# A fused gated-attention and expert-choice kernel: the second expert's weight halves, its copies, and one comparison of the routing, in another order

## The chip, the core and the metric

The kernel runs on one core of a Trainium2 chip. The metric is the device time of one launch in microseconds (us), the median of three runs. The profile is one further execution, recorded by the hardware profiler. The engines are PE (matrix products), DVE (vector), ACT (activations and copies), POOL (gathers, scatters and accumulating transfers) and SP (which only issues loads).

## The reference

A gated linear attention over q, k, v, alpha of shape (4 batches, 8 heads, 768 steps, 48) gives x, 3072 tokens by 384. x goes through a mixture of eight experts, each of which takes 384 tokens, in the order of all logits.

```python
for t in range(S):
    state = alpha[:, :, t, :, None] * state + np.einsum('bhd,bhe->bhde', k[:, :, t], v[:, :, t])
    y[:, :, t] = np.einsum('bhd,bhde->bhe', q[:, :, t], state)
...
logits = x @ w_gate
order = np.argsort(-logits.flatten())
for idx in order:
    tok, e = (int(idx) // E, int(idx) % E)
    if assigned[tok] >= 0 or counts[e] >= cap:
        continue
    assigned[tok] = e
    counts[e] += 1
    ...
for e in range(E):
    mask = assigned == e
    h = np.maximum(x[mask] @ w1[e], 0.0)
    out[mask] = h @ w2[e]
```

x is 3072 by 384, w_gate 384 by 8, w1 8 by 384 by 1024, w2 8 by 1024 by 384, all float32.

## The kernel before, in words

The kernel has two parts. The first computes the attention in 24 steps, writes x to memory (`x_dram`) and keeps the logits on the chip. The change does not touch it. The second does routing and experts, interleaved.

**Rounds.** A round of the routing finds the tokens of one expert. `search(i)` narrows down a threshold over the digits of the keys: DVE compares the digits with a ramp (`compare`, result `cmp`), PE counts with narrow matmuls (`rt`), DVE finds the digit (`gt`, `k`, `nd`), and so on for every digit. The first digit's comparison covers 128 x 3072 elements; those of later digits are smaller. `extract(i)` turns the choice into row numbers (`idx`, last line L905) and issues three gathers on POOL that fetch the 384 rows of x (`xr`, three blocks of 128). `update(i)` sets the logits of an expert that is full aside, makes new keys, and starts the next round with its first comparison. The first three rounds follow one another in priority, ahead of the experts' work; a later round is raised in priority at the place where its expert begins.

**Weights.** Each expert's w1 (384 by 1024) and w2 (1024 by 384) come in two halves of 768 KB each, raw into `w1r` and `w2r`, by loads that SP issues in `weights`. For experts from the third on both halves are asked for at once. For the first two, the second halves stand in a list `second_half`; `extract` issues them, with a dependency: w1's after gather 0 has landed, w2's after the last gather (gather 2).

**Splitting.** Matmuls work on a rounded high part and a rest. `split(i, hf)` makes both for one half of an expert's weights: ACT copies the rounded value (`w1hi`, `w2hi`) and its negative (`w1lo`, `w2lo`), each half in two pieces (L954); then POOL issues a transfer that adds the raw weights to the negated copy in memory (`low`, L942), and what is left in `w1lo` or `w2lo` is the rest. `behind(n)` names the instruction after which a piece's copies may be issued: for the second half of the first two experts the last `xh`, and the activations of hidden blocks 0, 2 and 3. For the rows of w2, each piece has its low copy and its high copy next to each other.

**Tokens.** `prep(i)` transposes the gathered rows on PE (`xt`, L991), ACT rounds them (`xh`, L994; the handle of the last is `XA[i]`), DVE takes the rest (`xl`, L996).

**Expert.** F = 1024 is worked through in eight hidden blocks of 128. `ffn1(i, q)` computes one with nine matmuls of 128 x 384 (`h`, L1007: high by high, high by rest, rest by high), then ACT makes the rounded ReLU (`hh`, L1011) and DVE its rest (`hl`, L1012). There are two PSUM buffers for `h`: the matmuls of a block wait until `hh` and `hl` of the block two before have read theirs. `ffn2(i, qs)` adds one hidden block to each of three output blocks of 128 tokens with three matmuls (`y`, L1027). After the eighth, ACT evacuates the output block (`yt`, L1031) and POOL scatters it to the output (L1038).

**Order.** The code of experts is written block by block: hidden block n, then the output matmuls of block n - 2. A list scheduler then gives each engine its order from priorities (order of writing, with routing raised) and modelled readiness; `tc.issue_after(x)` makes what is written inside it stand behind x. So an edit of one constraint can move rows elsewhere, and the tables below show what it does to the order.

Of the kernel before, what the change touches and what calls it, by code (L numbers as in the profile page):

```python
# [24 lines left out]
AF = mybir.ActivationFunctionType  # L25
OP = mybir.AluOpType
# [131 lines left out]
def gla_moe_kernel(ctx, tc, q, k, v, alpha, w_gate, w1, w2, out):  # L158
    nc = tc.nc
# [461 lines left out]
    def weights(i, ei):  # L621
        ev = nc.sync.value_load(ei[0:1, 0:1], min_val=0, max_val=E - 1)
        W1R[i] = wp.tile([128, DB, F], F32, name="w1r")
        W2R[i] = wp.tile([128, FB, Dm], F32, name="w2r")

        def load_w1(hf):
            fs = slice(hf * F // 2, (hf + 1) * F // 2)
            return nc.sync.dma_start(W1R[i][:, :, fs], w1v[bass.ds(ev, 1), :, :, fs].rearrange("e p c f -> p (e c) f"))

        def load_w2(hf):  # L630
            qs = slice(hf * FB // 2, (hf + 1) * FB // 2)
            return nc.sync.dma_start(W2R[i][:, qs], w2v[bass.ds(ev, 1), :, qs].rearrange("e p c d -> p (e c) d"))

        def half(hf):
            return load_w1(hf), load_w2(hf)

        half(0)
        if i > 1:
            half(1)
        else:  # L640
            second_half.extend((load_w1, load_w2))

    def compare(i, d, t):
        nt = 2 ** BITS[t]
# [150 lines left out]
    def update(i):  # L795
# [14 lines left out]
        if i + 2 < E:  # L810
            sg = rw.tile([128, NU], I32, name="sg")
            nc.vector.tensor_scalar(sg, m.bitcast(I32), 31, -2 ** 31, op0=OP.arith_shift_right,
                                    op1=OP.bitwise_or)
            nc.vector.scalar_tensor_tensor(asg, sel, es, asg, op0=OP.mult, op1=OP.add)
            key = rw.tile([128, NU], I32, name="key")
            nc.vector.tensor_tensor(key, m.bitcast(I32), sg, op=OP.bitwise_xor)
            val = rw.tile([128, NU, E], BF, name="val")
            nc.vector.tensor_tensor(val, lw, row(m, E), op=OP.is_equal)
            dig = rw.tile([128, nb, NU], BF, name="dig")
            digits(key, dig, rw, NU)  # L820
            st["dig"] = dig
            with tc.issue_after(st["idx"].ins) if i == 2 else ExitStack():
                for _ in compare(i + 1, dig[:, 0], 0):
                    pass
        else:
            nc.vector.scalar_tensor_tensor(asg, sel, es, asg, op0=OP.mult, op1=OP.add)
            val = rw.tile([128, NU, E], BF, name="val")
            nc.vector.tensor_tensor(val, lw, row(m, E), op=OP.is_equal)
# [34 lines left out]
    def extract(i):  # L863
# [49 lines left out]
                out=XR[i][:, b], out_offset=None, in_=x_dram,  # L913
                in_offset=bass.IndirectOffsetOnAxis(ap=IDX[i][:, b:b + 1], axis=0))

        for n, load_ in enumerate(second_half):
            tc.add_manual_dep(load_(1).ins, gathers[0 if n == 0 else NB - 1].ins.name,
                              mybir.DependencyInfo(mybir.DependencyClass.Sync, mybir.DependencyReason.DATA),
                              reason="rows of the first experts before their later weights")
        second_half.clear()  # L920
# [5 lines left out]
    def split(i, hf):  # L926
# [28 lines left out]

        for n, ix_ in enumerate(cols):
            copies(n, (hi1[ix_], w1r[ix_], 1.0), *([(lo1[ix_], w1r[ix_], -1.0)] * (not first)))
        for n, ix_ in enumerate(rows_):
            copies(2 + n, (lo2[ix_], w2r[ix_], -1.0), *([(hi2[ix_], w2r[ix_], 1.0)] * (not first)))
        if first:  # L960
            for ix_ in rows_:
                copies(0, (hi2[ix_], w2r[ix_], 1.0))
# [33 lines left out]
                nc.vector.tensor_sub(lo[:, :, bs], o, hi[:, :, bs])  # L996
        XH[i], XL[i] = hi, lo

    HH, HA, F1 = {}, {}, {}

    def ffn1(i, q):
        hi, lo = CH[i, q][:2]
        o = fps.tile([128, CAP], F32, name="h", bufs=2)
        n = 0
        for a, x in ((hi, XH[i]), (hi, XL[i]), (lo, XH[i])):
            for d in range(DB):
                F1[i, q] = nc.tensor.matmul(o, a[:, d], x[:, d], start=(n == 0), stop=(n == 3 * DB - 1))  # L1007
                n += 1
        hh = fp.tile([128, CAP], F32R, name="hh", bufs=4)
        hl = fp.tile([128, CAP], F32R, name="hl", bufs=4)  # L1010
        HA[i, q] = nc.scalar.activation(hh, o, AF.Relu)  # L1011
        nc.vector.scalar_tensor_tensor(hl, o, 0.0, hh, op0=OP.max, op1=OP.subtract)  # L1012
        HH[i, q] = hh, hl

    Y, F2 = {}, {}
# [1 line left out]
    def ffn2(i, qs):  # L1017
# [3 lines left out]
        for b in range(NB):  # L1021
            bs = slice(b * 128, (b + 1) * 128)
            for q in qs:
                hi, lo = CH[i, q][2:]
                hh, hl = HH[i, q]
                for n, (a, w) in enumerate(((hh, hi), (hh, lo), (hl, hi))):
                    F2[i, q] = nc.tensor.matmul(Y[b], a[:, bs], w,  # L1027
                                                start=(q == 0 and n == 0), stop=(q == FB - 1 and n == 2))
            if FB - 1 in qs:
                yt = fp.tile([128, Dm], F32, name="yt", bufs=5)  # L1030
                nc.scalar.activation(yt, Y[b], AF.Copy)  # L1031
                pending.append((i, b, yt))

    pending, scattered = [], []
# [11 lines left out]
    for n in range(E * FB + 2):  # L1046
        i, q = divmod(n, FB)
        if i < E:
            if q == 0:
                with tc.high_priority():  # L1050
# [5 lines left out]
                    search(i) if i < E - 1 else search_last(i)  # L1056
                    extract(i)
                    route_priority[0] = tc.cur_priority
                prep(i)
            if q % (FB // 2) == 0:  # L1060
                split(i, 2 * q // FB)
            ffn1(i, q)
        if n >= 2:
# [54 lines left out]
```

## Time and profile before

| | us |
|---|---|
| median of three runs | 418.32 |
| the runs | 417.75, 418.32, 418.52 |
| profiled execution | 418.74 |
| span of its trace | 417.0 |
| mean granted TensorE clock in it | 0.978 |
| busy PE | 390.9 (94%) |
| busy DVE | 282.7 (68%) |
| busy ACT | 215.2 (52%) |
| busy POOL | 190.1 (46%) |

The span runs from the first to the last instruction in the trace; the execution has 1.74 us around it. The times in the trace are counted from the span's start. In rows of the timeline stand the start, the duration, the engine, the line, the operation, and `result<-operands` by the program's names; `x3` means that three like it are drawn together; a bracket at the end holds how long the engine sat idle before, and what released it. SPq and POOLq are the sides of SP and POOL that issue transfers. In the view of transfers a row ends with the KB moved and the us from issue to landing. The clock is the share of full speed that PE was granted.

### The profile page before, as it was taken

To read this page: it belongs to the slowest core of one execution; us is meant where nothing else is said; L and a number is where in the kernel's file an instruction comes from. 1 tells how busy PE (TensorE), PEld (TensorE's weight loads), DVE (VectorE), ACT (ScalarE), POOL (GpSimd) and SP (SyncE) were. 2 spreads that over 40 slices of the span, in tenths; PEclk is the share of its full clock that TensorE was granted. 3 is DMA by queue.
4 is the path that set the end of the run, shared out by engine and by line. 5 is a ranking of instruction groups with operands and counts; after the bars stand their busy time and mean duration, and the time that the engine had idled before them with its cause. 6 is when DMAs were issued, how large, how long until landed. Compare 5 with 4: busy or idle time off the path is not lost.

```text
span 417.0 us, 10031 instructions
## 1 busy us (share of the span) xinstructions
PE 390.9 (94%) x3883; PEld 347.4 (83%) x3883; DVE 282.7 (68%) x849; ACT 215.2 (52%) x382; POOL 190.1 (46%) x209
## 2 busy tenths in 40 slices
PE   7899999999999889989959999999999999999992
PEld 3788889877897547978858999898998999999992
DVE  8889998899984696695783797786966941312210
ACT  3456556645652026456536529529628539568211
POOL 4799988666841025144234117245252263614102
PEclk9899999999999999999995999999999999999997
DMA  8989898762022059769899965999998999989601
GB/s 283 362 276 318 264 317 241 236 186 98 18 78 78 2 183 236 149 211 232 222 243 302 210 237 174 193 261 326 211 326 213 209 323 351 241 226 194 157 0 57
DMA packets 43711, 88.05 MB, mean 211 GB/s; under 512 B 3856, under 2 KB 18192, under 8 KB 43664
## 3 DMA queue, kind: packets, MB, share of 16 engines
q1 hardware_dynamic: 32256, 53.60, 38.1%
q0 software_dynamic: 11408, 33.83, 38.1%
q8 instruction: 30, 0.49, 0.5%
q14 instruction: 17, 0.14, 0.1%
HBM read 53.59 MB, written 9.44 MB: 151 GB/s over the span
## 4 chain that ended last, share of the span: by engine, by line
PE 55%; issue 14%; DVE 14%; DMA 12%; POOL 3%; ACT 0%; POOLq 0%; DVEq 0%; ACTq 0%
PE h L1007 14%; PE y L1027 13%; PE xt L391 4%; PE s L403 4%; PE y L454 4%; DMA w1lo<-w1r 4%; PE y L447 4%; DMA w2r<-in_moe_w_dram 3%; DMA w2lo<-w2r 3%; DVE te L363 2%; PE rt L707 2%; PE lg L472 2%; PE rt L710 2%; DVE tp L369 2%; POOL out_dram L1038 2%
## 5 line engine op out<-in xcount | busy, mean ns | idle before, releaser
L1011 ACT ACTIVATE hh<-h 128x384 fp32r<-128x384 f32 x64 | 31.3, 489 | 89.5 <-PE h L1007 73.5
L1027 PE MATMUL y<-w2lo,hh 128*128 128x384 f32 x192 | 65.8, 343 | 4.1 <-DMA w2lo<-w2r 4.1
L1012 DVE SCALAR_TENSOR_TENSOR hl<-h,hh 128x384 fp32r<-128x384 f32 x64 | 35.2, 553 | 50.5 <-ACT hh L1011 50.0
L1027 PE MATMUL y<-w2hi,hh 128*128 128x384 f32 x192 | 66.8, 348 | 0.0
L1027 PE MATMUL y<-w2hi,hl 128*128 128x384 f32 x192 | 65.5, 347 | 0.0
L912 POOL DMA_INDIRECT xr<-x_dram,idx x24 | 32.1, 1338 | 57.3 <-DVE idx L905 22.8
L1007 PE MATMUL h<-xh,w1hi 128*128 128x384 f32 x192 | 47.2, 350 | 1.9 <-DVE hl L1012 1.9
L1007 PE MATMUL h<-xh,w1lo 128*128 128x384 f32 x192 | 47.3, 346 | 0.3 <-DMA w1lo<-w1r 0.3
L1038 POOL DMA_INDIRECT out_dram<-yt,idx x24 | 24.8, 1032 | 48.5 <-ACT yt L1031 44.6
L1007 PE MATMUL h<-xl,w1hi 128*128 128x384 f32 x192 | 46.4, 347 | 0.0
L1027 PEld LDWEIGHTS y<-w2lo,hh 128*128 128x128 f32 x192 | 36.6, 191 | 4.4 <-DMA w2lo<-w2r 4.4
L942 POOL DMA_DIRECT2D w1lo<-w1r x15 | 20.6, 1372 | 41.2 <-ACT w1lo L954 39.3
L373 POOL TENSOR_TENSOR kh<-rk,te 128x512 f32<-128x512 f32 (+1 forms) x24 | 29.4, 1227 | 18.7 <-DVE z L383 11.3
L1007 PEld LDWEIGHTS h<-xh,w1hi 128*128 128x128 f32 x192 | 34.1, 193 | 3.4 <-DVE hl L1012 2.2
L1027 PEld LDWEIGHTS y<-w2hi,hh 128*128 128x128 f32 x192 | 36.6, 191 | 0.0
L1027 PEld LDWEIGHTS y<-w2hi,hl 128*128 128x128 f32 x192 | 36.5, 191 | 0.1
L1007 PEld LDWEIGHTS h<-xl,w1hi 128*128 128x128 f32 x192 | 34.7, 193 | 0.8 <-DVE xl L996 0.2
L1007 PEld LDWEIGHTS h<-xh,w1lo 128*128 128x128 f32 x192 | 34.5, 191 | 0.5 <-DMA w1lo<-w1r 0.4
L650 DVE TENSOR_TENSOR cmp<-nd,iota 128x1536 bf16<-128x1536 bf16 (+3 forms) x32 | 32.7, 1032 | 0.9
L405 ACT ACTIVATE sm<-s 128x1024 f32<-128x1024 f32 x24 | 24.6, 1024 | 14.0 <-PE s L403 13.8
L369 DVE TENSOR_TENSOR_SCAN tp<-al,z 128x512 f32<-128x512 f32 (+1 forms) x26 | 29.6, 1138 | 2.6 <-DVE z L383 0.5
L363 DVE TENSOR_TENSOR_SCAN te<-al,z 128x511 f32<-128x511 f32 (+2 forms) x26 | 30.9, 1187 | 0.5
(191 smaller groups left out, 830.8 us busy)
## 6 DMA issues: line engine op xcount, KB each, us to landing
w1r<-in_moe_w_dram SPq DMA_DIRECT2D x16, 768.0 KB, 12.6
w2r<-in_moe_w_dram SPq DMA_DIRECT2D x16, 768.0 KB, 14.1
w2lo<-w2r POOLq DMA_DIRECT2D x16, 768.0 KB, 10.7
w1lo<-w1r POOLq DMA_DIRECT2D x15, 768.0 KB, 8.9
al<-in_alpha_dram SPq DMA_DIRECT2D x24, 260.0 KB, 4.2
rk<-in_k_dram SPq DMA_DIRECT2D x24, 256.0 KB, 4.3
rq<-in_q_dram SPq DMA_DIRECT2D x24, 256.0 KB, 4.4
rv<-in_v_dram SPq DMA_DIRECT2D x24, 192.0 KB, 4.1
```

The lines of the kernel that those rows point to most:

```text
L363: nc.vector.tensor_tensor_scan(te.t[:, lo:top][:, ::-1], al.t[:, lo + 1:top + 1][:, ::-1], zb[:, lo + 1:top + 1][:, ::-1], al.t[:, 4 * C + ...
L369: nc.vector.tensor_tensor_scan(tp.t[:, lo:hi], al.t[:, lo:hi], zb[:, lo:hi], 1.0, op0=OP.mult, op1=OP.add)
L373: eng.tensor_tensor(out_.t[:, us].rearrange("p u c -> p (u c)"), x.t[:, lo:hi], f.t[:, lo:hi], op=OP.mult)
L405: add(A_, 1.05, lambda: nc.scalar.activation(sm.t, sc.t, AF.Copy), r=[(sc, 0), (sc, 1)], w=[sm])
L650: nc.vector.tensor_tensor(words(dst, nt, js), keyed(d, nt, js), each(iotas[t], nt, js), op=OP.is_ge)
L912: gathers[b] = last_gather[0] = nc.gpsimd.indirect_dma_start(out=XR[i][:, b], out_offset=None, in_=x_dram, in_offset=bass.IndirectOffsetOn ...
L942: return nc.gpsimd.dma_start(x.bitcast(F32), raw_, accum_op=OP.add, max_dma_last_dim=8192)
L1007: F1[i, q] = nc.tensor.matmul(o, a[:, d], x[:, d], start=(n == 0), stop=(n == 3 * DB - 1))
L1011: HA[i, q] = nc.scalar.activation(hh, o, AF.Relu)
L1012: nc.vector.scalar_tensor_tensor(hl, o, 0.0, hh, op0=OP.max, op1=OP.subtract)
L1027: F2[i, q] = nc.tensor.matmul(Y[b], a[:, bs], w, start=(q == 0 and n == 0), stop=(q == FB - 1 and n == 2))
L1038: st_ = nc.gpsimd.indirect_dma_start(out=out, out_offset=bass.IndirectOffsetOnAxis(ap=IDX[i][:, b:b + 1], axis=0), in_=yt, in_offset=None)
```

## The change

1. `weights`: for the second expert (i = 1), w1's second half is asked for at once, behind the first halves of w1 and w2, and w2's second half after gather 0 in place of gather 2. The first expert keeps its order.
2. `update(1)`: the first comparison of the third round (of expert 2, counted from 0) stands behind `hl` of the first expert's seventh hidden block. `ffn1` keeps the handle of `hl` in `HL` for that.
3. `split(1, 1)`: the copies of w2 are listed as both low copies (behind hidden block 2's activation) and then both high copies (behind block 3's), in place of low and high for each piece.
4. `ffn2`: the first expert's evacuations stand behind the second expert's last `xh`.
5. The main loop calls `split(1, 0)` ahead of `prep(1)`, not behind it.

```diff
--- before.py
+++ after.py
@@ -637,8 +637,11 @@
         half(0)
         if i > 1:
             half(1)
+        elif i:
+            load_w1(1)
+            second_half.append((load_w2, 0))
         else:
-            second_half.extend((load_w1, load_w2))
+            second_half.extend(((load_w1, 0), (load_w2, NB - 1)))
 
     def compare(i, d, t):
         nt = 2 ** BITS[t]
@@ -819,7 +822,8 @@
             dig = rw.tile([128, nb, NU], BF, name="dig")
             digits(key, dig, rw, NU)
             st["dig"] = dig
-            with tc.issue_after(st["idx"].ins) if i == 2 else ExitStack():
+            behind = {1: HL.get((0, FB - 2)), 2: st["idx"]}.get(i)
+            with tc.issue_after(behind.ins) if behind is not None else ExitStack():
                 for _ in compare(i + 1, dig[:, 0], 0):
                     pass
         else:
@@ -913,8 +917,8 @@
                 out=XR[i][:, b], out_offset=None, in_=x_dram,
                 in_offset=bass.IndirectOffsetOnAxis(ap=IDX[i][:, b:b + 1], axis=0))
 
-        for n, load_ in enumerate(second_half):
-            tc.add_manual_dep(load_(1).ins, gathers[0 if n == 0 else NB - 1].ins.name,
+        for load_, b in second_half:
+            tc.add_manual_dep(load_(1).ins, gathers[b].ins.name,
                               mybir.DependencyInfo(mybir.DependencyClass.Sync, mybir.DependencyReason.DATA),
                               reason="rows of the first experts before their later weights")
         second_half.clear()
@@ -955,8 +959,12 @@
 
         for n, ix_ in enumerate(cols):
             copies(n, (hi1[ix_], w1r[ix_], 1.0), *([(lo1[ix_], w1r[ix_], -1.0)] * (not first)))
-        for n, ix_ in enumerate(rows_):
-            copies(2 + n, (lo2[ix_], w2r[ix_], -1.0), *([(hi2[ix_], w2r[ix_], 1.0)] * (not first)))
+        if i == 1 and hf:
+            copies(2, *((lo2[ix_], w2r[ix_], -1.0) for ix_ in rows_))
+            copies(3, *((hi2[ix_], w2r[ix_], 1.0) for ix_ in rows_))
+        else:
+            for n, ix_ in enumerate(rows_):
+                copies(2 + n, (lo2[ix_], w2r[ix_], -1.0), *([(hi2[ix_], w2r[ix_], 1.0)] * (not first)))
         if first:
             for ix_ in rows_:
                 copies(0, (hi2[ix_], w2r[ix_], 1.0))
@@ -996,7 +1004,7 @@
                 nc.vector.tensor_sub(lo[:, :, bs], o, hi[:, :, bs])
         XH[i], XL[i] = hi, lo
 
-    HH, HA, F1 = {}, {}, {}
+    HH, HA, F1, HL = {}, {}, {}, {}
 
     def ffn1(i, q):
         hi, lo = CH[i, q][:2]
@@ -1009,7 +1017,7 @@
         hh = fp.tile([128, CAP], F32R, name="hh", bufs=4)
         hl = fp.tile([128, CAP], F32R, name="hl", bufs=4)
         HA[i, q] = nc.scalar.activation(hh, o, AF.Relu)
-        nc.vector.scalar_tensor_tensor(hl, o, 0.0, hh, op0=OP.max, op1=OP.subtract)
+        HL[i, q] = nc.vector.scalar_tensor_tensor(hl, o, 0.0, hh, op0=OP.max, op1=OP.subtract)
         HH[i, q] = hh, hl
 
     Y, F2 = {}, {}
@@ -1028,7 +1036,8 @@
                                                 start=(q == 0 and n == 0), stop=(q == FB - 1 and n == 2))
             if FB - 1 in qs:
                 yt = fp.tile([128, Dm], F32, name="yt", bufs=5)
-                nc.scalar.activation(yt, Y[b], AF.Copy)
+                with tc.issue_after(XA[1].ins) if i == 0 else ExitStack():
+                    nc.scalar.activation(yt, Y[b], AF.Copy)
                 pending.append((i, b, yt))
 
     pending, scattered = [], []
@@ -1056,8 +1065,10 @@
                     search(i) if i < E - 1 else search_last(i)
                     extract(i)
                     route_priority[0] = tc.cur_priority
+                if i == 1:
+                    split(i, 0)
                 prep(i)
-            if q % (FB // 2) == 0:
+            if q % (FB // 2) == 0 and n != FB:
                 split(i, 2 * q // FB)
             ffn1(i, q)
         if n >= 2:
```

What this does to the order is shown at three places. The first is DVE around the first comparison of the third round, `cmp_101<-dig`, while the first expert's last hidden blocks are worked on; `chu`, `rem` and `o` are the last steps of `update`, `gt` and `k` the search's next ones. Before:

```order
L836 TENSOR_TENSOR chu<-ch,un 128x24
L837 SCALAR_TENSOR_TENSOR rem<-cl,rem 128x8
L650 TENSOR_TENSOR cmp_101<-dig,iota 128x3072
L839 TENSOR_TENSOR o<-ramp_b,chu 128x192
L1012 SCALAR_TENSOR_TENSOR hl<-h,hh 128x384 x2
L717 TENSOR_TENSOR gt_97<-rt,rem 128x8
L729 TENSOR_REDUCE k<-rt 128x1
```

And after:

```order
L840 TENSOR_TENSOR chu<-ch,un 128x24
L841 SCALAR_TENSOR_TENSOR rem<-cl,rem 128x8
L1020 SCALAR_TENSOR_TENSOR hl<-h,hh 128x384
L843 TENSOR_TENSOR o<-ramp_b,chu 128x192
L1020 SCALAR_TENSOR_TENSOR hl<-h,hh 128x384
L653 TENSOR_TENSOR cmp_101<-dig,iota 128x3072
L1020 SCALAR_TENSOR_TENSOR hl<-h,hh 128x384
L720 TENSOR_TENSOR gt_97<-rt,rem 128x8
L732 TENSOR_REDUCE k<-rt 128x1
```

Two residuals now stand ahead of the comparison. In two later rounds the order moves one residual the other way, from ahead of the round's `sums` or `lw` to behind that round's first comparison.

The second place is ACT at the second expert's second half of weights (`w2lo`, `w2hi`; `hh` are activations of its hidden blocks, `yt` the last evacuation of the first expert). Before:

```order
L1031 ACTIVATE yt<-y_2284 128x384
L1011 ACTIVATE hh<-h 128x384
L954 ACTIVATE w2lo<-w2r 128x768
L954 ACTIVATE w2hi<-w2r 128x768
L1011 ACTIVATE hh<-h 128x384
L954 ACTIVATE w2lo<-w2r 128x768
L954 ACTIVATE w2hi<-w2r 128x768
L1011 ACTIVATE hh<-h 128x384
```

And after:

```order
L1019 ACTIVATE hh<-h 128x384
L958 ACTIVATE w1lo<-w1r 128x3x256
L1019 ACTIVATE hh<-h 128x384
L958 ACTIVATE w2lo<-w2r 128x768 x2
L1019 ACTIVATE hh<-h 128x384
L958 ACTIVATE w2hi<-w2r 128x768 x2
L1019 ACTIVATE hh<-h 128x384 x2
```

Both low copies now follow one activation; the last evacuation has moved up, ahead of the copies of w1. On POOL all three scatters of the first expert now stand ahead of the second half's accumulate into `w1lo`; before, it was two, and one behind it.

The third place is PE at the second expert's second and third hidden block (`y_2284` is the first expert's last output block, `y_2768` the second expert's first). Before:

```order
L725 LDWEIGHTS one_84
L725 MATMUL rt<-gt_97,one_84 128x8
L1007 MATMUL h<-xh,w1lo 128x384 x2
L1027 MATMUL y_2284<-w2lo,hh 128x384
L1027 MATMUL y_2284<-w2hi,hl 128x384
L1007 MATMUL h<-xh,w1hi 128x384 x3
L1007 MATMUL h<-xl,w1hi 128x384 x2
```

And after:

```order
L728 LDWEIGHTS one_84
L728 MATMUL rt<-gt_97,one_84 128x8
L1015 MATMUL h<-xh,w1lo 128x384 x3
L1035 MATMUL y_2768<-w2hi,hh 128x384
L1035 MATMUL y_2768<-w2lo,hh 128x384
L1015 MATMUL h<-xh,w1hi 128x384 x3
L1015 MATMUL h<-xl,w1hi 128x384 x3
```

The first expert's output matmuls are all done earlier, ahead of the second expert's first hidden block, and the second expert's own first two have taken their place. A little earlier on PE, the transposes of the second expert's first block stand ahead of the 24 narrow matmuls of the comparison; before, they followed them.

## The prediction

> **What bounds the kernel now.** I read the page's busy times first, then TensorE's (PE's) waits by what ended them, then busy time in single stretches beside the granted clock, and last the timeline around each wait.
>
> ```profile
> PE 390.9 (94%) x3883; PEld 347.4 (83%) x3883; DVE 282.7 (68%) x849; ACT 215.2 (52%) x382; POOL 190.1 (46%) x209
> ```
> PE is busy for 94% of the span, so only PE's idle time and its clock can be won. In the part from 120 us to the end, where all edits lie, the waits of the expert matmuls are these three (us in total, times, longest):
> ```profile
> PE y L1027 <- DMA w2lo<-w2r: 4.1, 1, 4.1
> PE h L1007 <- DVE hl L1012: 1.9, 1, 1.9
> PE h L1007 <- DMA w1lo<-w1r: 0.3, 1, 0.3
> ```
> The next view gives, for a stretch, its length, the busy time of PE, weight load, DVE, ACT and POOL, the granted clock, the DMA share and GB/s:
> ```profile
> 9.37:12.79 3.42, 1.45 (x28) 1.14 (x25) 3.27 (x9) 1.40 (x4) 2.91 (x4) 1.00 1.08 382
> 12.79:16.20 3.41, 3.41 (x30) 2.71 (x25) 3.24 (x8) 0.64 (x2) 2.31 (x3) 0.50 1.05 367
> 183.45:186.87 3.42, 1.92 (x11) 1.60 (x10) 3.42 (x12) 3.42 (x5) 3.12 (x2) 1.00 0.71 254
> 214.17:217.59 3.42, 0.75 (x5) 0.43 (x3) 2.99 (x5) 2.49 (x4) 2.61 (x2) 1.00 1.05 233
> 217.59:227.83 10.24, 8.84 (x49) 7.92 (x50) 2.89 (x5) 6.46 (x9) 4.16 (x4) 0.50 1.07 313
> 342.00:390.00 48.00, 48.00 (x292) 47.08 (x291) 12.01 (x25) 35.05 (x59) 18.80 (x18) 1.00 1.03 254
> ```
> The wait of 4.1 us costs twice: behind the window that it empties (0.75 of 3.42 busy) PE runs at half clock for 10.24 us, and 8.84 us of work there would have taken half, 4.42 us. The last row shows the later experts: no idle, nothing to win, but any new delay is paid in full. The start 12.79 and the start 217.59 of the half clock lie 204.8 us apart, 60 times 3.413: the clock is decided in fixed windows of that length. A window 0.42 busy (1.45 of 3.42) lost the clock, one 0.56 busy (1.92) kept it. I take the threshold between, at 1.5 to 2.0 us idle in one window.
>
> The Trainium skill, "TensorE: Matmul & The Clock Gate", section "Why this matters for your kernels", asks for no PE gap above about 3 us, since one window of idle brings the half clock back. The 4.07 us wait agrees with that; the first window, with 28 matmuls in it, loses the clock all the same, so the measurement is the stricter one. By the page alone, no wait that I expect below would cost clock, and rival A would fall away.
>
> **The change, part by part.** All against the profiled execution, 418.74 us (span 417.0, 1.74 around it); the median is 418.32, 0.42 lower.
>
> *Comparison behind a residual.* Now the third round's first comparison stands ahead of two residuals on DVE, and the eighth hidden block's matmuls wait for one of them:
> ```profile
> 184.73 1.75 DVE L650 TENSOR_TENSOR cmp<-dig,iota 128x3072 bf16<-128x3072 bf16 x1
> 186.67 1.01 DVE L1012 SCALAR_TENSOR_TENSOR hl<-h,hh 128x384 fp32r<-128x384 f32 x2
> 187.28 0.79 PE L1007 MATMUL h<-xh,w1hi 128*128 128x384 f32 x3 [1.91 <-DVE hl L1012]
> ```
> The new order has two residuals first, about 1.0 us; the 1.75 us comparison no longer stands in PE's way: **+1.91** (1.5 to 1.91). The comparison itself comes about 1 us later; behind it on DVE stand the round's next steps, whose matmuls are filled in between expert matmuls.
>
> *Request order and copies.* The second expert's second halves, now:
> ```profile
> 187.06 0.37 SPq L628 DMA_DIRECT2D w1r<-in_moe_w_dram  x1
> 191.82 0.37 SPq L632 DMA_DIRECT2D w2r<-in_moe_w_dram  x1
> w2r<-in_moe_w_dram SPq DMA_DIRECT2D x1, 768.0 KB, 13.1
> 201.92 0.49 ACT L1011 ACTIVATE hh<-h 128x384 fp32r<-128x384 f32 x1 [1.58 <-PE rt L725]
> 205.04 0.84 ACT L954 ACTIVATE w2lo<-w2r 128x768 fp32r<-128x768 f32 x1 [2.63 <-DMA w2r<-in_moe_w_dram]
> 208.04 0.91 POOL L942 DMA_DIRECT2D w2lo<-w2r  x1 [5.56 <-ACT w2lo L954]
> w2lo<-w2r POOLq DMA_DIRECT2D x1, 768.0 KB, 10.9
> 218.99 0.69 PE L1027 MATMUL y<-w2lo,hh 128*128 128x384 f32 x1 [4.07 <-DMA w2lo<-w2r]
> ```
> The w2 load leaves SP when the third gather lands (191.82) and arrives at 204.9 (13.1 later). With gather 0 as its condition it leaves at 187.06, where w1's left, and by the same 13.1 arrives by 200.2. ACT then needs only the activation that the copies stand behind (201.92, done 202.41) and the two low copies side by side (2 x 0.84): POOL can issue at 204.1 instead of 208.04. At the same 10.9 the low half lands at 215.0, where PE wants it at 218.99 - 4.07 = 214.92. PE's own gains move both ends alike. So **+4.07** (3.4 to 4.07), and the high copies, now last, follow one activation later, still long before that use. With the wait the emptied window goes, and the half clock: **+4.42** (0 to 4.42, nothing if another window takes its place).
>
> *w1's second half at once.* SP sends it right behind the first halves, ahead of the gathers of x:
> ```profile
> w1r<-in_moe_w_dram SPq DMA_DIRECT2D x1, 768.0 KB, 4.7
> w2r<-in_moe_w_dram SPq DMA_DIRECT2D x1, 768.0 KB, 6.2
> 181.98 1.09 POOL L912 DMA_INDIRECT xr<-x_dram,idx  x1 [8.06 <-DVE idx L905]
> xr<-x_dram,idx POOLq DMA_INDIRECT x1, 5.1
> 188.95 0.96 PE L707 MATMUL rt<-o,cmp 128*128 128x8 bf16 x24
> 190.50 0.82 PE L991 MATMUL xt<-ident,xr 128*128 128x128 f32 x6
> ```
> The second of two loads took 1.5 us more than the first (6.2 against 4.7), so gather 0 may land up to 1.5 us after its 187.1 (181.98 + 5.1). The first transposes now stand ahead of the 24 narrow matmuls and reach PE at 190.50 - 1.91 - 0.96 = 187.6. **-0.5** (0 to 1.0). The w2 load's start moves with that gather; at 1.5 us later it still arrives before 201.92.
>
> *Split and evacuations.* The first expert's three evacuations stand behind the third xh now, and the new order puts no output matmuls between the last transposes and the second expert's first hidden block (four before):
> ```profile
> 194.19 0.49 PE L991 MATMUL xt<-ident,xr 128*128 128x128 f32 x3
> 195.33 0.77 PE L1007 MATMUL h<-xh,w1hi 128*128 128x384 f32 x3
> ```
> From the transposes' end (194.68) to the matmul that uses their xh (195.33): **-0.65** (0.3 to 0.7), uncovered. Next, the second expert's first two output matmuls stand ahead of its third hidden block instead of behind it:
> ```profile
> 188.92 1.06 POOL L942 DMA_DIRECT2D w2lo<-w2r  x1
> w2lo<-w2r POOLq DMA_DIRECT2D x1, 768.0 KB, 11.7
> 202.02 0.34 PE L1027 MATMUL y<-w2lo,hh 128*128 128x384 f32 x1
> ```
> They reach PE at about 202.02 - 2.0 (nine wide at 48.00 / 292 = 0.164, and twelve narrow at 0.04) - 0.76 (1.91 less the 1.15 above) = 199.3; the low half lands at 188.92 + 11.7 = 200.6 at the latest. **-1.2** (0 to 1.9). The third scatter now stands ahead of the low half of w1 on POOL, and that half's 0.3 us wait could stay or double: **-0.3** (0 to 0.7).
>
> *What is late next.* PE reaches the third expert sooner, its weights don't come sooner: their low halves are issued behind gathers that follow the round's idx.
> ```profile
> 214.24 0.16 DVE L905 SCALAR_TENSOR_TENSOR idx<-xt,other 64x3 int32<-64x3 f32 x1
> 219.67 1.46 POOL L942 DMA_DIRECT2D w1lo<-w1r  x1
> w1lo<-w1r POOLq DMA_DIRECT2D x1, 768.0 KB, 10.2
> 236.74 0.34 PE L1007 MATMUL h<-xh,w1lo 128*128 128x384 f32 x1
> 252.10 0.16 DVE L905 SCALAR_TENSOR_TENSOR idx<-xt,other 64x3 int32<-64x3 f32 x1
> 258.15 1.44 POOL L942 DMA_DIRECT2D w1lo<-w1r  x1
> w1lo<-w1r POOLq DMA_DIRECT2D x1, 768.0 KB, 6.9
> ```
> From idx to use it is 22.5 us now; both big gains fall inside it (8.5), and the new order leaves 7 wide and 12 narrow matmuls fewer in between (1.6): 12.3. From idx to landing took 15.6 here (5.4 + 10.2) and 13.0 for the fourth expert (6.0 + 6.9). So a new wait of 0.7 to 3.3; I take a little above the middle, since the first row is the same expert: **-2.2**. In two later rounds the new DVE order moves one residual from ahead of the round's sums to behind the first comparison, as it stood in the case just mended:
> ```profile
> 300.21 1.76 DVE L650 TENSOR_TENSOR cmp<-dig,iota 128x3072 bf16<-128x3072 bf16 x1
> ```
> Each may cost nothing or a comparison's 1.8; I take 1.7 for the one at this row and half, 0.8, for the earlier one: **-2.5** (0 to 3.6).
>
> Sum: 1.91 + 4.07 + 4.42 = 10.40 won; 0.5 + 0.65 + 1.2 + 0.3 + 2.2 + 2.5 = 7.35 given back; net 3.05. 418.74 - 3.05 = 415.7 for a profiled execution, **415.3** on the median. Half-widths added in squares give 2.5 to either side: 412.8 to 417.8.
>
> **Rivals.**
> A, the half clock comes back. The new wait at the third expert's first low half empties a window. It decides where 1.5 to 2.0 us of one window are idle; then three windows at half clock cost about 4.4 again: 415.3 + 4.4 = 419.7, slower. For it: a wait of 2.2 us lies in a window at random, and has 1.75 of it in one window with a chance of (3.41 - 2.2 + 2 x 0.45) / 3.41 = 0.6. Against: only about half of the waits that I allow there are that long.
> B, most waits that I fear are covered: the later residuals cost nothing (2.5 back) and the third expert's weights come as fast as the fourth's did (0.6 instead of 2.2). Net 7.15: 411.2. For it: the later rows at 342 to 390 show no idle at all under the same structure. Against: the 1.91 us case is just such a residual.
> C, the change doesn't do what it says: the w2 load, though sooner asked for, arrives no sooner, since it shares the DMAs with w1's half and the low accumulates (shares of 1.05 and 1.07 in the windows above), or the low half takes 4 us longer in flight. Then the 4.07 and 4.42 stay, and 1.91 pays for 0.5 + 0.65 + 0.3, and for the rest little is asked since PE is as late as before: 418.3.
>
> **How the numbers follow.** Three runs from 417.75 to 418.52 tell 0.2%, 0.84 us, from no change: "same" is 417.5 to 419.2. Forecast 0.53 (0.50 of it faster, 0.03 same); A 0.27, since half of the 0.8 that B and C leave, times 0.6, is about a quarter (spread 417.0 to 420.8: 0.05 faster, 0.09 same, 0.13 slower); B 0.13, faster; C 0.07 (0.04 same, 0.03 slower). Faster 0.68, same 0.16, slower 0.16. The range 411.0 to 420.0 leaves out some 0.05 of B, 0.08 of A and 0.03 of the forecast.
>
> **What the changed profile would show.** Right: no wait of h on hl near 185; the w2 load of the second expert leaving near 187, two low copies in a row on ACT, and the low accumulate issued before 205; no y wait on w2lo above 0.7 and a clock of 1.00 from 214 to 225; a wait of h on w1lo of about 2 us at the third expert. Wrong: slices of half clock anywhere after 180 (A); no wait above 0.5 after 222 (B); the 4 us wait still there (C). What would upset all of it is a wait on the gathers near 187 longer than 1 us, because everything of the second expert stands behind it.

## The result, and the profile after

In the first set of runs the changed kernel took 420.29 us (median of 20, 417.74 to 422.80) against 417.12 us of the kernel before (20 runs, 413.45 to 422.49): a ratio of 1.0092, interval 1.0067 to 1.0117. The forecast was 415.3 us. Two more sets of runs gave 0.9999 (0.9968 to 1.0029) and 1.0032 (0.9997 to 1.0067). The kernel before, run against itself, gave 1.0005, 0.9944 and 0.9991, so a set of runs can be off by some 0.5%. The ratios leave out runs more than 1.5% above the fastest of their kernel and aren't quotients of the medians; by the medians of all runs the three sets of the change give 1.0076, 0.9981 and 1.0009. So no set shows a gain clear of noise, and the first shows a loss of 0.8 to 0.9%.

The profiled execution of the changed kernel took 417.74 us (span 416.0), the shortest of its 20; that of the kernel before, 418.74, lies 1.6 above the median of the 20 runs. The two profiles alone would say "1 us faster".

From the page of the profile after, busy times and the granted clock in 40 equal slices of the span (a digit is tenths of full speed, 9 is 90% or more):
```profile
PE 388.0 (93%) x3883; PEld 345.2 (83%) x3883; DVE 282.7 (68%) x849; ACT 214.2 (51%) x382; POOL 189.7 (46%) x209
PEclk9899999999999999999999998999999999999997
```
The waits of PE after, from 120 us on (us in total, times, longest), those of the experts and rounds that grew or are new:
```profile
PE rt L710 <- DVE cmp L653: 3.7, 1, 3.7
PE h L1015 <- DVE hl L1020: 1.3, 1, 1.3
PE xt L999 <- DMA xr<-x_dram,idx: 1.2, 1, 1.2
PE y L1035 <- DMA w2lo<-w2r: 0.7, 1, 0.7
PE h L1015 <- ACT xh L1002: 0.6, 1, 0.6
```
The waits of 4.1 and 1.9 us are gone, and five others of 7.5 us in all stand in their place. The residual first (timeline after):
```profile
185.11 0.79 PE L1015 MATMUL h<-xh,w1hi 128*128 128x384 f32 x3
185.71 1.74 DVE L653 TENSOR_TENSOR cmp<-dig,iota 128x3072 bf16<-128x3072 bf16 x1
```
The hidden block starts before the comparison does. Then the low half of w2, request to use:
```profile
188.65 0.37 SPq L632 DMA_DIRECT2D w2r<-in_moe_w_dram  x1
203.37 1.57 ACT L958 ACTIVATE w2lo<-w2r 128x768 fp32r<-128x768 f32 x2
205.25 0.93 POOL L946 DMA_DIRECT2D w2lo<-w2r  x1 [2.54 <-ACT w2lo L958]
w2lo<-w2r POOLq DMA_DIRECT2D x1, 768.0 KB, 7.1
216.72 0.33 PE L1035 MATMUL y<-w2lo,hh 128*128 128x384 f32 x1
```
The two low copies stand together, the accumulate leaves 2.8 us sooner than before (208.04) and lands at 212.3, 4.4 us ahead of its use. The new large wait lies in the round of the fifth expert (the fourth expert's row numbers, and the second digit's comparison behind them), while the third expert is computed. PE, ACT and DVE there, in order of time:
```profile
244.60 0.68 PE L1015 MATMUL h<-xh,w1lo 128*128 128x384 f32 x3
245.58 0.85 ACT L958 ACTIVATE w1hi<-w1r 128x768 fp32r<-128x768 f32 x1 [4.33 <-DMA w1r<-in_moe_w_dram]
249.27 0.46 ACT L1019 ACTIVATE hh<-h 128x384 fp32r<-128x384 f32 x1
249.76 0.56 DVE L1020 SCALAR_TENSOR_TENSOR hl<-h,hh 128x384 fp32r<-128x384 f32 x1 [4.37 <-ACT hh L1019]
250.91 0.16 DVE L909 SCALAR_TENSOR_TENSOR idx<-xt,other 64x3 int32<-64x3 f32 x1
251.11 1.76 DVE L653 TENSOR_TENSOR cmp<-nd,iota 128x3072 bf16<-128x3072 bf16 x1
252.92 0.96 PE L710 MATMUL rt<-o,cmp 128*128 128x8 bf16 x24 [3.65 <-DVE cmp L653]
```
The hidden block is complete at 245.3. ACT serves it at 249.27, because five of the fourth expert's copies stand ahead in ACT's queue: the first waits 4.33 us for its raw weights, and the five then take from 245.58 to 249.27. Before, the same five copies started at 249.81 without a wait and ended at 253.49, when a hidden block had just been completed (253.16). The residual waits for that activation, the row numbers stand behind the residual on DVE, the comparison behind the row numbers, and PE stands in front of the counts of that comparison. The clock follows; busy times and clock by windows:
```profile
246.68:250.09 3.41, 2.59 (x15) 2.27 (x14) 0.33 (x1) 3.41 (x6) 1.16 (x1) 1.00 1.04 384
250.09:253.51 3.42, 0.59 (x17) 0.59 (x18) 3.06 (x7) 3.42 (x6) 2.38 (x2) 1.00 0.94 183
253.51:256.92 3.41, 3.41 (x22) 3.10 (x20) 1.37 (x5) 2.46 (x4) 2.81 (x4) 0.50 0.88 201
```

### The profile page after: what moved, and what is told of

Read it like the earlier page. It is cut to its first block, busy times and chain, and to the rows that moved or that the text cites. A ratio compares the mean times of both kernels' runs of the same rounds, so it can differ in the third digit from the quotient of the medians.

```text
span 416.0 us, 10032 instructions
## 1 busy us (share of the span) xinstructions
PE 388.0 (93%) x3883; PEld 345.2 (83%) x3883; DVE 282.7 (68%) x849; ACT 214.2 (51%) x382; POOL 189.7 (46%) x209
## 4 chain that ended last, share of the span: by engine, by line
PE 52%; DVE 17%; issue 14%; DMA 10%; POOL 3%; ACT 1%; POOLq 0%; SPq 0%; DVEq 0%; ACTq 0%
PE h L1015 13%; PE y L1035 12%; PE xt L391 4%; PE y L447 4%; PE y L454 4%; DMA w1lo<-w1r 4%; PE s L403 4%; DMA w1r<-in_moe_w_dram 3%; DMA w2lo<-w2r 3%; DVE te L363 3%; PE lg L472 2%; PE rt L710 2%; PE rt L713 2%; DVE tp L369 2%; POOL out_dram L1047 2%
## 5 line engine op out<-in xcount | busy, mean ns | idle before, releaser
L916 POOL DMA_INDIRECT xr<-x_dram,idx x24 | 30.6, 1275 | 57.9 <-DVE idx L909 29.4
L1047 POOL DMA_INDIRECT out_dram<-yt,idx x24 | 25.8, 1074 | 48.6 <-ACT yt L1040 44.4
L1015 PE MATMUL h<-xl,w1hi 128*128 128x384 f32 x192 | 45.1, 340 | 0.0
L958 ACT ACTIVATE w1hi<-w1r 128x768 fp32r<-128x768 f32 x32 | 26.8, 840 | 9.8 <-DMA w1r<-in_moe_w_dram 7.4
```

The costliest lines, as they stand in the source:

```text
L916: gathers[b] = last_gather[0] = nc.gpsimd.indirect_dma_start(out=XR[i][:, b], out_offset=None, in_=x_dram, in_offset=bass.IndirectOffsetOn ...
L958: nc.scalar.activation(dst, src, AF.Copy, scale=scale)
L1047: st_ = nc.gpsimd.indirect_dma_start(out=out, out_offset=bass.IndirectOffsetOnAxis(ap=IDX[i][:, b:b + 1], axis=0), in_=yt, in_offset=None)
```

## The experiments

All are timed against the kernel before in the same set of runs. Two figures help to read them. The clock loss of a run is 1 minus its mean granted clock, times its span: the time that a PE that is always busy loses to half clock. The rest is the run's time less that. The table has the medians of both over all runs. The waits are those of PE on experts and rounds from 176 to 400 us, added up in the one trace of each kernel.

| kernel | median, before in the same set | ratio (interval) | clock loss | rest | waits |
|---|---|---|---|---|---|
| loads_copies | 419.91, 422.49 | 0.9952 (0.9919 to 0.9985) | 7.1 | 413.8 | 6.9 |
| residual_only | 421.78, 422.49 | 0.9997 (0.9961 to 1.0033) | 5.9 | 415.8 | 9.2 |
| all_but_residual | 421.09, 422.49 | 0.9977 (0.9940 to 1.0014) | 8.2 | 413.5 | 7.0 |
| change_again | 421.68, 422.49 | 0.9999 (0.9968 to 1.0029) | 6.5 | 416.2 | 8.5 |
| before_again | 422.26, 422.24 | 1.0005 (0.9959 to 1.0052) | 10.1 | 412.8 | 7.1 |
| change_copies_later | 420.05, 422.24 | 0.9967 (0.9935 to 0.9999) | 5.9 | 414.3 | 7.6 |
| loads_copies_later | 423.24, 422.24 | 1.0028 (0.9989 to 1.0067) | 9.1 | 414.3 | 9.0 |
| before_copies_later | 427.55, 422.24 | 1.0152 (1.0104 to 1.0200) | 10.2 | 417.5 | 10.6 |
| change_w1_behind_gather | 421.97, 417.70 | 1.0101 (1.0052 to 1.0150) | 8.2 | 413.8 | 9.1 |
| change_all_copies_later | 419.02, 417.70 | 1.0022 (0.9986 to 1.0059) | 6.1 | 413.0 | 6.5 |
| change_sixth_residual | 418.10, 417.70 | 1.0012 (0.9981 to 1.0043) | 5.8 | 412.7 | 5.8 |
| change_all_three | 419.29, 417.70 | 1.0066 (1.0029 to 1.0103) | 7.5 | 412.1 | 6.2 |
| change_two_placements | 414.61, 418.38 | 0.9915 (0.9877 to 0.9953) | 3.7 | 410.8 | 3.4 |
| change_third | 418.76, 418.38 | 1.0032 (0.9997 to 1.0067) | 6.0 | 413.3 | 6.8 |
| loads_copies_again | 416.66, 418.38 | 0.9960 (0.9914 to 1.0006) | 5.6 | 410.3 | 4.5 |
| before_third | 416.65, 418.38 | 0.9944 (0.9892 to 0.9996) | 6.2 | 410.7 | 4.7 |
| two_placements_again | 416.15, 422.18 | 0.9884 (0.9823 to 0.9946) | 4.8 | 411.7 | 5.2 |
| before_fourth | 421.87, 422.18 | 0.9991 (0.9951 to 1.0031) | 8.8 | 413.0 | 6.9 |

There were six sets of runs. In three of them the kernel before takes 422.2 to 422.5 us, in the others 417.1 to 418.4; the last section says what the traces show of that. The chip alone doesn't explain it: two sets are recorded on chip 3, and before takes 417.70 us in one and 422.18 in the other. The difference isn't the same for every kernel, so ratios of different sets are compared with care.

### Which part moves the order

In the programs' order, the new requests and the paired copies alone leave PE and DVE as they were before. The comparison behind the residual alone changes both, in later rounds too: counted from the first expert, the row numbers of the fourth, fifth and sixth expert then stand behind 22, 29 and 35 residuals on DVE, before behind 21, 28 and 34. So the first four kernels part the two.

**Loads and copies alone** (`weights`, `extract` and the copies of `split` from the change, all else from before).

> Only the request order of the second expert's loads and its paired low copies; the order on PE and DVE stays that of before. Theory 1 (the loss comes from the order that the comparison behind a residual brings to the fourth expert's round, where row numbers and the second digit's comparison now stand behind one more residual): the 4.07 us wait on w2lo goes with its half clock, the 1.91 us wait on the residual stays, no wait on a comparison above 0.5 us near 250; 3 to 6 us faster than before. Theory 2 (whatever PE gains early is given back to later weights and rounds): the 4 us go, but waits of the same sum appear behind 220; within 1.5 us of before.

**Residual alone** (`behind` in `update`, with `HL`).

> Only the comparison behind the residual; loads, copies, evacuations and split as before. Theory 1: the 1.91 us wait is gone, the 4 us wait on w2lo stays with its half clock, and near 250 PE waits 1 to 3.7 us for the second digit's comparison; 0 to 3 us slower than before. Theory 2: nothing but the 1.91 us changes; 1 to 2 us faster.

**All but the residual** (`update` as before, the rest as in the change).

> The whole change without the comparison behind the residual. Theory 1: as with loads and copies alone, 3 to 6 us faster than before, so 6 to 9 faster than the whole change; no wait on a comparison near 250. Theory 2: near the whole change, 1 to 4 us slower than before, with waits on weights or row numbers behind 220.

**The whole change again.**

> The whole change once more, for a second trace. Theory 1: the wait of 3 to 4 us on the second digit's comparison near 250 is there again, and half clock follows it; 2 to 4 us slower than before. Theory 3 (which windows the clock loses is chance, and no wait of the change's own decides): the wait is there or not, and the half clock lies at other places; the time differs from the first profile's by up to 4 us.

The residual alone took 1.9 us less wait at its place and more elsewhere: rest 415.8 against before's 413.5 in that set (35 runs). The new waits are 3.0 us on the second expert's w1 low half near 198, 1.6 behind a residual at 224 and 1.9 on the comparison near 255. The wait on w2lo, expected to stay, is gone. Loads and copies alone were faster, by 2.6 us where 3 to 6 were expected, and all but the residual by 1.4, within the bounds of no change. So theory 1 was right on the side that makes things worse, but most of the wait that loads and copies remove comes back too, with the old order: 6.9 us of waits in all, against 7.1 in before_again. The largest of those that are new, in the timeline of loads_copies:
```profile
246.27 0.85 ACT L957 ACTIVATE w1hi<-w1r 128x768 fp32r<-128x768 f32 x1 [2.47 <-DMA w1r<-in_moe_w_dram]
249.96 0.47 ACT L1017 ACTIVATE hh<-h 128x384 fp32r<-128x384 f32 x1
250.46 0.56 DVE L1018 SCALAR_TENSOR_TENSOR hl<-h,hh 128x384 fp32r<-128x384 f32 x1 [2.53 <-ACT hh L1017]
250.93 0.15 DVE L720 TENSOR_TENSOR gt<-rt,rem 128x8 bf16<-128x8 f32 x1
251.14 0.17 PE L728 MATMUL rt<-gt,one 128*128 128x8 bf16 x1 [1.45 <-DVE gt L720]
```
It is the same ACT queue: copies that wait for the fourth expert's raw weights hold up an activation, that a residual, that a step of the round. In the old order only `gt` stands behind that residual, since the row numbers came one residual sooner; in the new one the row numbers and the comparison do, and the price is 3.0 to 3.7 us in place of 1.45. In the first trace of before PE completes that hidden block 8 us later (253.16 against 245.28) and waits for nothing.

### Is it the copies on ACT?

One number changes, for the fourth expert (i = 3):
```diff
-            return HA[i - 1, SPLIT_AFTER[i > 1]] if i and not hf else None
+            return HA[i - 1, 5 if i == 3 else SPLIT_AFTER[i > 1]] if i and not hf else None
```
`SPLIT_AFTER[1]` is 4, so the copies now follow the activation that they held up.

> The kernel before once more, for a second trace. Both theories below: the 4.07 us wait on w2lo near 215 and the 1.9 us wait on the residual are there again, and no wait above 1 us between 240 and 260. How long the half clock lasts behind the first is open: 3.4 us (one window) or 10.2 us (three); if it differs from trace to trace, the time of this kernel varies by some 3 us for that alone.

> The whole change, and the fourth expert's weight copies (first half) stand behind the third expert's sixth activation on ACT in place of its fifth. Theory A (those copies, waiting for weights that land near 245.6, keep the sixth activation waiting on ACT, it the residual on DVE, that the row numbers and the second digit's comparison, and PE): the wait of 3 to 3.7 us near 250 falls below 1 us and its half clock goes; 3 to 6 us faster than the whole change, so 2 to 6 us faster than before. Theory B (the round itself takes that long once PE is early, whatever ACT does): the wait stays above 2 us or shows at the next step of the same round; within 1.5 us of the whole change.

> Loads and paired copies alone, with the same one placement of the fourth expert's copies. Theory A: the 1.45 us wait near 251 goes with its window of half clock; 1.5 to 4 us faster than loads and copies alone, so 3 to 6 us faster than before. Theory B: a wait of 1 us or more stays at that round; within 1 us of loads and copies alone.

> The kernel before with that one placement and nothing else. Theory A: PE reaches the fourth expert's round some 8 us later there and never waits for it, so within 1 us of before. If the placement is good by itself, whatever PE does: 2 us or more faster than before.

In the changed kernel the wait near 250 is gone, as theory A says, and the time fell from 0.9999 to 0.9967 of before's; that is 1.4 us, not 3 to 6, and across two sets. A wait with the same cause came one expert later, since the fifth expert's copies wait 3.22 us for their weights on ACT:
```profile
281.24 0.17 PE L728 MATMUL rt<-gt,one 128*128 128x8 bf16 x1 [2.21 <-DVE gt L720]
```
With the old order the same edit does harm: in loads_copies_later and before_copies_later it moves a residual behind a comparison, and a new wait of 2.35 us on `hl` stands at 268 and 275. Theory A's "within 1 us" for before was wrong: it became 5.3 us slower, since the edit moves PE's and DVE's order also where no wait was. Loads and copies alone, for which 1.5 to 4 us of gain were expected, lost too. This pair doesn't test the cause; the changed kernel does.

### Each wait at its own place

Three edits on the whole change, one by one and together:
```diff
-            load_w1(1)
-            second_half.append((load_w2, 0))
+            second_half.extend(((load_w1, 0), (load_w2, 0)))
```
```diff
-            return HA[i - 1, SPLIT_AFTER[i > 1]] if i and not hf else None
+            return HA[i - 1, 5 if i > 2 else SPLIT_AFTER[i > 1]] if i and not hf else None
```
```diff
-            behind = {1: HL.get((0, FB - 2)), 2: st["idx"]}.get(i)
+            behind = {1: HL.get((0, FB - 2)), 2: st["idx"], 5: HL.get((4, 0))}.get(i)
```

> The whole change, but the second expert's second half of w1 is asked for behind gather 0 again (w2's second half right after it); the order on every other engine is that of the change. Theory A (each wait stands where its own cause is, and leaves with it): the wait of 1.2 to 1.4 us on the gathered rows near 189 goes and no other grows; 1 to 1.5 us faster than the whole change. Theory B (what is won at one place is waited for at the next routing step or weight): within 0.7 us of the whole change, or slower, with a wait on w1lo or w2lo near 205 to 217.

> The whole change, with the copies of the first half of every expert from the fourth on placed one activation later (the fourth alone was tried before and moved a wait of 2.2 us to 281). Theory A: no wait above 1 us at 250 or at 281; 3 to 5 us faster than the whole change. Theory B: a wait of 1 to 3 us stays at one of these rounds, or weights come too late for their first use; within 1.5 us of the version with the fourth expert's copies alone, or slower than it.

> The whole change, with the same placement for the round of the seventh expert: its first comparison behind the fifth expert's first residual. Theory A: the wait of 1.3 us on that residual near 302 goes, the one near 250 stays; 1 to 1.5 us faster than the whole change. Theory B: the later comparison makes the round late, and PE waits at 305 to 312 for it by 1 us or more over the whole change; within 0.7 us of it.

> The three edits together on the whole change. Theory A: the gains add to 5 to 8 us, so 1 to 2% faster than before. Theory B: no better than the best of the three alone, within 1.5 us.

The early request earns its keep: without it the wait on the gathered rows falls from 1.2 to 0.3, but w1's low half comes late, and theory B is right there (waits of change_w1_behind_gather):
```profile
PE h L1014 <- DMA w1lo<-w1r: 3.1, 1, 3.1
PE xt L998 <- DMA xr<-x_dram,idx: 0.3, 1, 0.3
```
The two placements do to the waits what theory A says: with the copies later no wait stands at 250 or 281 (2.4 us on a low half of w1 at 354 instead), with the residual of the seventh expert's round none at 302; at 1.0022 and 1.0012 both lie 0.7 to 0.8% under the 1.0092 of the whole change, but only 0.1 to 0.2% under its 1.0032, all from different sets. So what each is worth alone isn't shown, and the 3 to 5 us expected of the copies didn't come. All three together came out at 1.0066, where 1 to 2% of gain was expected: the missing early request costs 3.1 us at 199, and the copies, late for a later expert as at 354 above, 2.0 at 357.

### Both placements, and the clock

The copies one activation later for the fourth to sixth expert (`5 if 2 < i < 6`), and the third edit above; the early request stays.

> The whole change, with the copies of the fourth to sixth expert's first halves one activation later and the seventh expert's first comparison behind the fifth expert's first residual. Theory C (the change's loss is its new waits near 250 and 302; the clock costs both kernels about the same): both waits below 0.7 us; 3 to 5 us faster than the whole change, so 0 to 1% faster than before. Theory D (each wait removed comes back later): waits of the same sum behind 270; within 1.5 us of the whole change.

> The whole change a third time. Theory C: median loss by half clock (1 minus the mean clock, times the span) within 1 us of that of the kernel before on this chip, and the rest of the time 2 to 3 us longer than before's. If the forecast's clock term holds: the loss is 3 us or more below before's.

> Loads and paired copies alone, again. Theory C: no new order, so no new waits near 189 and 302, and 1.5 us near 251; 0 to 3 us faster than before. If all of the change's early gain is paid back whatever the order: slower than before by 1 us or more, like the whole change.

> The kernel before a third time, for its trace on the same chip. Theory C: the wait on w2lo is 2.8 to 4.1 us, and the half clock behind it one to two windows of 3.4 us rather than three.

One set of runs now holds both kernels with their traces. The kernel before: its waits, and the windows around them.
```profile
PE y L1027 <- DMA w2lo<-w2r: 2.8, 1, 2.8
PE h L1007 <- DVE hl L1012: 1.9, 1, 1.9
```
```profile
184.05:187.46 3.41, 1.51 (x9) 1.19 (x8) 3.21 (x7) 3.41 (x6) 3.16 (x2) 1.00 0.38 120
187.46:190.87 3.41, 3.41 (x34) 2.97 (x32) 0.17 (x1) 1.90 (x3) 2.10 (x2) 0.50 0.84 262
214.77:218.18 3.41, 0.62 (x5) 0.31 (x3) 3.17 (x6) 2.55 (x4) 2.45 (x1) 1.00 1.00 277
218.18:225.01 6.83, 6.83 (x43) 6.22 (x44) 2.58 (x5) 4.55 (x7) 4.31 (x4) 0.50 1.07 368
```
The changed kernel, third trace:
```profile
PE rt L710 <- DVE cmp L653: 3.0, 1, 3.0
PE h L1015 <- DVE hl L1020: 1.3, 1, 1.3
PE xt L999 <- DMA xr<-x_dram,idx: 1.3, 1, 1.3
PE y L1035 <- DMA w2lo<-w2r: 0.6, 1, 0.6
PE h L1015 <- ACT xh L1002: 0.6, 1, 0.6
```
4.7 us of waits before, 6.8 after: 2.1 more. The rest, without clock loss, is 411.1 for before (35 runs) and 413.3 for the change: 2.2 more. The clock loss is 6.7 and 6.0: 0.6 less. So theory C holds in this set: the change pays more in waits and wins next to nothing in clock. In the set of change_again the rest is 2.7 more (416.2 against 413.5) and the clock loss 1.9 less (6.5 against 8.4): more in clock, and still no gain. The wait on w2lo was 2.8 us here (2.9 and 2.6 in the other two repeats), not 4.07, and the half clock behind it two windows, not three.

With both placements, these are all the waits that are listed:
```profile
PE xt L999 <- DMA xr<-x_dram,idx: 1.0, 1, 1.0
PE xt L999 <- DVE xl L1004: 0.8, 1, 0.8
PE y L1035 <- DMA w2lo<-w2r: 0.7, 1, 0.7
PE h L1015 <- ACT xh L1002: 0.6, 1, 0.6
PE h L1015 <- DMA w1lo<-w1r: 0.3, 1, 0.3
```
3.4 us in place of 6.8, no half clock between 16 and 408 us, and 414.61 us: 4.2 under the whole change, 3.8 under before. The expectation was 3 to 5 under the change. In this set the kernel before, against itself, came out at 0.9944, so part of the 0.9915 may be noise. A repeat in another set confirms the gain:

> The version with both placements again. Theory C (waits near 250 and 302 gone, so the early gain is kept): 0.5 to 1.5% faster than before, waits on PE behind 176 us of 3 to 4.5 us in all and a median loss by half clock 2 us or more below before's. If the first comparison was chance: within 0.4% of before.

> The kernel before against itself: within 0.4% if runs of the same kernel on one chip agree, up to 0.6% off if not. Waits of 1.9 and 2.8 to 4.1 us as in its other traces.

0.9884 (0.9823 to 0.9946) against before, with before against itself at 0.9991. The clock loss is 3.6 us below before's (4.8 against 8.4), where 2 or more was expected; the waits are 5.2 us, where 3 to 4.5 were. Loads and copies alone, at 0.9960 in their second set and 0.9952 in the first, may be worth having by themselves, but 0.4 to 0.5% is no more than a set of runs can be off.

## Why the prediction was wrong, point by point

- **Residual, +1.91.** Right: PE no longer waits for `hl` near 185.
- **Low half of w2, +4.07.** Right in mechanism. The accumulate left at 205.25 (204.1 forecast) and took 7.1 us where 10.9 were assumed. The wait that it removed is 2.6 to 2.9 us in three other traces of before, so the term was also too big by some 1.2.
- **Half clock, +4.42.** This is the step that failed: about 0.6 us was gained in the set that has both kernels' traces (1.9 in the set of change_again). The half clock behind the wait is real. It is in all four traces of before, 10.24 us in the first and 6.8 to 6.9 in the others, and in none of the three of the change. But in each of those three another window, 3.41 us at half clock, stands behind the new wait near 250, which gives back up to 1.7 us. And the term took the half clock of one execution for that of the kernel: the profiled execution had a clock of 0.978, a loss of 9.2 us, where the median loss of before is 6.7 in the sets in which it takes about 418 us; single runs in the set of change_third lose from 2.1 to 13.5. The change's own median loss is 6.0 in such a set, and 7.1 in the first. The 2.5 us (9.2 - 6.7) and the 1.7 are together an estimate of why the term was some 3.8 too big. The range of the term, 0 to 4.42, was stated, but left to rival A: the half-widths added in squares give 2.5 only without it, and 3.4 with it.
- **Gathers, -0.5 (0 to 1.0).** Under-sized: 1.2 to 1.4 us, since the w1 load ahead of them held up gather 0. It lands at the time at which w2's load leaves, 188.65 in the timeline, where 187.1 to 188.6 was allowed. A wait above 1 us here was to upset the whole forecast; without the early request it fell to 0.3, but the kernel got no faster.
- **xh, -0.65, first use of w2's low half, -1.2, w1's low half, -0.3.** 0.57, 0.6 to 0.7, and 0. Together 0.9 better than forecast.
- **Third expert's first low half, -2.2.** It didn't come:
```profile
221.39 1.44 POOL L946 DMA_DIRECT2D w1lo<-w1r  x1
w1lo<-w1r POOLq DMA_DIRECT2D x1, 768.0 KB, 6.7
228.47 0.68 PE L1015 MATMUL h<-xh,w1lo 128*128 128x384 f32 x3
```
  It landed at 228.1, 0.4 us ahead of its use; the flight took 6.7 us, close to the 6.9 of the fourth expert before, and not the 10.2 that was weighed most. From idx (215.94) to this use it was 12.5 us, where 12.3 was forecast; to landing 12.2, where 13.0 to 15.6 was.
- **Later residuals, -2.5 (0 to 3.6).** At the one near 302, 1.3 us against 1.7. At the earlier one 3.0 to 3.7 against 0.8, by another cause than forecast: it isn't a residual behind a comparison but ACT's queue, in which copies wait for weights that come no sooner while PE does.

The waits given back were forecast at 7.35 us in all and measured at 7.5 in the first trace, by terms that were wrong in both directions, so that this agreement is luck. Without the clock term the same sum says 1.91 + 4.07 - 7.35 = -1.4, slower: 419.7 on the median. Rival A came nearest, with half clock behind a new wait and 419.7 us, but it put the wait at the third expert's weights, where it was in the fifth expert's round, and charged three windows, where one followed. Its threshold holds only roughly: the forecast's row of 183.45 was 0.56 busy and kept the clock, but in loads_copies the window at 248.71 was 0.57 busy (1.96 of 3.41) and lost it. Before_third's window of 184.05, with the same 1.9 us wait as the forecast's row, was 0.44 busy (1.51 of 3.41) and lost it: one wait costs clock or not as it falls in a window. Rival C's 418.3 us is the time of a profiled execution; on the median, as the others are given, it would be 417.9.

The Trainium skill, "TensorE: Matmul & The Clock Gate", Part 1, calls that window free-running, with a transition that varies from run to run. The traces agree: the first half clock starts at 12.79 us in the first trace of before, at 10.9 in the second, and not at all near there in the third. The rule of no gap above about 3 us, in the Trainium skill's "TensorE: Matmul & The Clock Gate", section "Why this matters for your kernels", doesn't hold here: in before_third a wait of 1.9 us cost a window.

## What to carry to other kernels

A clock loss read from one profiled execution is a draw: price it by the granted clocks of many runs, and let the sum stand on the waits alone. When a change brings the bound engine forward, follow the engines that serve it in their fixed order; an in-order queue with a copy that waits for a load holds up whatever stands behind it, and the first place where that was just hidden is where the gain goes. Moving two placements with the change made it worth 0.9 to 1.2%.

## What the hardware showed that was not expected

In some sets of runs every trace has one count after which DVE's next step starts late, in others none has. In loads_copies, PE's counts and DVE's next step (`remote` in a bracket: the view names no engine that released it):
```profile
304.98 0.96 PE L710 MATMUL rt<-o,cmp 128*128 128x8 bf16 x24
308.59 0.17 DVE L720 TENSOR_TENSOR gt<-rt,rem 128x8 bf16<-128x8 f32 x1 [4.70 <-remote]
308.81 0.17 PE L728 MATMUL rt<-gt,one 128*128 128x8 bf16 x1 [2.41 <-DVE gt L720]
```
and in loads_copies_again, the same program in another set:
```profile
305.83 0.96 PE L710 MATMUL rt<-o,cmp 128*128 128x8 bf16 x24
306.83 0.17 DVE L720 TENSOR_TENSOR gt<-rt,rem 128x8 bf16<-128x8 f32 x1 [2.15 <-PE rt L710]
```
The step follows the counts' end by 2.65 us in the first (304.98 + 0.96 = 305.94 to 308.59) and by 0.04 in the second. In these sets it costs the order of before 2.3 to 2.45 us of PE's time, that of the change 1.0 to 1.4, and is as large as most of what before's rest differs by between sets (413.5 to 413.8 against 411.1). The change loses some 1 us less to it than before does, 0.25%, which fits its ratio of 0.9999 in a set that has it against 1.0032 in one without; it doesn't reach to the 1.0092 of the first set. What holds the step up isn't known, the signal from PE or something else; no experiment was aimed at it.
